# Roots on GpSimd, MLP token groups without shared buffers, early statistics for half of q, two halved tables, and transposes of h by DMA

## The chip, the cores and the metric

One core of a Trainium2 chip runs the kernel. The metric is the device time of one execution in microseconds. A core has five engines with queues of their own: TensorE (PE, with its weight loads shown apart as PEld), VectorE (DVE), ScalarE (ACT), GpSimd (POOL) and SyncE (SP), which here does nothing but issue DMAs. They meet only at semaphores.

## What is computed

A layer norm, a gated long convolution, and a mixer with an MLP, on 2048 tokens of 512 channels in bf16, one batch:

```python
h  = x + q_n * y,         x = q,  q_n = layernorm(q)
     kv = (causal 4-tap filter of k, per channel) * v
     y  = irfft(rfft(pad(kv)) * rfft(pad(ssm_k)))[:S] + kv * ssm_D
n  = layernorm(h)
g  = gelu(layernorm(n) @ w1)      # 512 -> 512
x1 = n + shifted(g) @ w2          # four channel quarters moved by +1, -1, +2, -2 tokens
h2 = gelu(layernorm(x1) @ w3) @ w4   # 512 -> 1792 -> 512
out = h + x1 + h2
```

## The kernel before

**Order by hand.** The kernel does not run its steps in the order of the code. Each call of `add`, `v` or `dma` appends a step to a list, with the engines that may run it (A for ACT, V for DVE, G for GpSimd, S for SP), an estimate of its duration and the names that it reads and writes. `Plan.issue` then emits the steps in the order of the numbers in `ISSUE` (L40 to L72); a number is the step's place in the list, and a letter behind it picks the engine where there is a choice. Every engine runs its own instructions in that order, so each engine's queue can be read off the string.

**Front.** k, v and the convolution kernel h (`ssm_k`) are loaded; k's tiles are transposed on PE, and the four taps are products with diagonal matrices (L399), accumulated in PSUM and multiplied by v on DVE (L404). Sixteen DMAs (L412) put these rows into the layout of the transform. Beside this, GpSimd, DVE and ACT make tables of sines and cosines: iota, a multiply and add (L306), an AND (L309), a sine (L313 to L320), and four DMAs scatter a table into `Wc` (L354). h is transposed on PE (L427) and evacuated into `Rh`.

**Transform.** Stage A (L446) transforms k and h in 16 blocks each; each block is cast from PSUM into `Tk` or `Th` on ACT (L161) or DVE (L163). Stage C (L470 to L473) gives spectra in 32 blocks, cast into `xt`; `product` (L586 to L593) multiplies the two spectra on DVE in eight chunks, the last two in halves. Then 16 blocks on PE (L647) are cast into `Gs`, and `last_level` (L702) gives y for two token tiles at a time.

**Norms.** q (a norm of 16 tiles) is loaded whole after h's buffer is free; DVE takes `bn_stats` and `bn_aggr` of each tile (L552, L553), and a Newton iteration of eight DVE instructions (L532 to L537), with one or two ahead and one behind, gives the reciprocal roots. ACT and DVE apply them (L632, L635). `gate` multiplies y by the normalized q, adds q and takes statistics; after every second pair of tiles `rsqrt_h` (Newton for two roots at once, since layer norm is applied twice) and four normalizations give `hn`; `on_pe` transposes it, two tiles at a time, and ACT or DVE evacuates it.

**MLP.** `gelu_mm` is one block of 128 hidden channels for 512 tokens: four matmuls of 512 columns and a gelu on ACT. `mix` adds the product with w2 to the normalized h (L834), takes statistics and a third set of roots, normalizes, and transposes: the first token group on PE, the other three by DMA from SP (L861). w3 and w4 follow for the token groups 2 to 5, 6 to 9, 10 to 13, and 14, 15, 0, 1.

**Buffers.** Large tiles share slots by tag (`slot`): a new tile in a slot waits for the readers of the old one. k, v and k's rows share C; in turn `Yp` and then the MLP's activations take it. y's scratch `ysb` lies in the tile of the weights, in the place that the output's scratch uses later; `x1` takes the slot of the normalized q.

Of the kernel before, what the change touches and what calls it, by code (L numbers as in the profile page):

```python
# [16 lines left out]
P = 128  # L17
# [23 lines left out]
25 3 0 5 7 4 1 2 49 9 26 8 11 29 24 21 6 50V 31 23 13 10 51 16 85 32G 14 22 52 12 20 86V 87 48 15 19 40 74 17 98  # L41
88A 27 34 46 108 35V 99A 37 75 91 109V 53 36 89 39 92 66 76G 28 102 67 90 33 97 100 93 103 62 18 128 30 94 57G
96 47 131 68 101 133 64 38 107 134 132V 104 42 69 105 95 44 63 106 65 77 118 78V 41 79 135V 110 80 54G 83 58 84
45 59 55 112 60 43 119V 129 70 113 71 73 72 111 136 130A 81 117 82 115 122 114 212 137A 120 123 56 61 200 121
138 210 179 201A 208 211V 186 126 209A 127 196 124 187V 197A 206 125 184 116 213 207A 185V 188 214 182 189A 183V
180 139 190 181A 204 202 140G 205V 191A 155 156A 203V 153 163 154A 147 164V 173 148A 174V 151 149 152A 167 141
169 150A 168V 171 170A 177 172V 159 178A 198 160V 175 199A 157 176V 158A 161 192 223 162A 165 239 257 166A 243
194 235 258 195A 261 224 241 193A 259 245 225 142 263 244 260V 265 262A 143 240 237 266A 273 219 144G 264A 275
221 217 277 274A 267 271 276A 289 238 268 272A 287 246 270 278A 283 215 290A 269 285 229 284A 297 280 288A 279
286A 295 236 282 298A 299 281 301 296A 233 313 291 302A 307 292 300A 309 230 294 314A 311 293 308A 242 304 310A  # L50
319 303 312A 321 222 306 325 320A 305 323 231 322A 315 326A 337 316 324A 331 234 317 338A 335 318 332A 333 218
327 345 336A 328 347 334A 343 227 346A 329 349 420 330 348A 385 363 366 226 340 365 344A 339 367 364 228 342
350A 341 145 352 146 351 220 354 353 232 396 216 355 247 356 394 397A 248 358 398 249 357 395A 250 360 359 399A
390 251 400 362 368 391A 252 361 392 253 401V 414 393A 406 254 407V 416 415A 404 417A 255 405V 410 402 411A 408
256 403V 388 409A 386 389V 387A 412 379V 421 413A 380V 371V 373V 370A 418 422 369V 382A 383V 374V 384V 430 378V
423A 372V 375V 381A 424 457 431A 425 428 376A 465 432 458A 426 433 466A 492 429 434 419 500 436 435 427 437 467
377A 438 493A 501A 527 459 441A 468 442A 460 443A 445 469 444A 463 535 446A 470 471 689 464 528A 461 447 472 462
494 448A 473 536A 455 502 477A 495 476A 503 479A 480 496 453 478A 537 481A 449 498 506 454 482 504 456 483A 507
499 451 497 505 538 450 508 486 452 488 487 490 541 512A 484 539 489 511V 491 529 515 485 474 568 530 516A 569
542 531 514A 513V 533 517 532 572 534 540 518A 439 475 543 521 525 440 546A 547V 509 570 522 550 510 571 526 523  # L60
551A 549V 519 548V 575 524 552 520 577 553A 573 595 578 574 579 556 581 554 557 580 576 582 583 558 555 560 559
592 596 585A 584V 561 597 587A 588 594 615 589A 586V 593 565 590 617 618 591A 600 601 544 616 714 562 716 566
715 567 564 692 545 717 563 598 696 693 599 604 690 605 602 698 647 699 697 691 704 649 708 619 705 603 712 606
709 706 713 702 707 607V 700 620 703 608 609V 710 701 648 610 694 711 623 650 627 695 624 613A 718 719 614 653
611V 621 612 625 622 626 628 629 630 651 631 652 659 657 734 658 660 728 671 632 655 735 633 736 654 723 729 738
634 635 672 724 673 674 675 676 636 637 638 645V 639A 643V 646 739 640 737 644 750 725 752 751 677 727 678 742
679 753 680 641V 720 730 642 743 726 748 731 656 722 661 662 732 663 721 685V 749 756 686 744 733 740 687V 745
761 688 754 741 664 746 665 755 666 667 668 788 669 747 670 681V 770 762 771 789 786 763 768 787 799 778 784 779
683V 769 684 757 682 785 764 765 824 758 780 825 759 794 772 781 760 782 773 766 783 774 767 792 775 790 793 776
791 818 777 826 819 804 827 806 805 828 807 820 829 830 821 812 831 800 813 814 801 808 815 822 809 810 816 811  # L70
823 795 817 833 796 832 798 802 803 797 838 834 837 836 835 842 839 841 840 843 844 845
# [3 lines left out]
class Plan:  # L75
# [5 lines left out]
    LAT = 0.2  # L81
# [40 lines left out]
def kernel(  # L122
# [48 lines left out]
    slot("C", [P, 24064], "kin")  # L171
    slot("S1", [P, DC, S], "hraw")
    slot("B", [P, 11776], "kta")
# [4 lines left out]
    def k_sb():  # L178
        return X["kin"][:, 0:9728].rearrange("p (r d) -> p r d", d=D)

    def v_sb():
        return X["kin"][:, 9728:15872].rearrange("p (b t d) -> p b t d", b=3, d=D)

    def Rk():
        return X["kin"][:, 15872:24064].rearrange("p (n d) -> p n d", d=2 * P)

    def kT():
        return X["kta"][:, 0:9728].rearrange("p (c r s) -> p c r s", c=DC, s=P)

    def dg():  # L190
        return X["kta"][:, 9728:11776].rearrange("p (c j s) -> p c j s", c=DC, s=P)
# [741 lines left out]
```

## Time and profile before

| | us |
|---|---|
| median of three runs (261.11 to 263.3) | 261.93 |
| profiled execution | 262.43 |
| its span, first to last instruction | 260.4 |

PE is busy for 227.0 us, DVE for 180.7, ACT for 152.7 and GpSimd for 30.0. Mean durations of single instructions, ns:

| what | engine, line | ns, count |
|---|---|---|
| Tk, Th, xt, Gs casts, 128x1024 from PSUM | ACT L161 | 1034 to 1064 |
| the same | DVE L163 | 1187 to 1231 |
| product, 128x2048 | DVE L586 | 1213, 12 |
| statistics of a tile, aggregate | DVE L552, L553 | 677 to 681, 163 to 170 |
| normalization of a tile | ACT L740, DVE L635 | 805, 406 |
| gelu block | ACT L772 | 596, 56 |
| matmul of 512 columns | PE L768 | 383; successive ones start 216 apart |
| eight transposes of h or x at full clock | PE L756 | 455 for eight in the chain of waits |
| iota in three levels | GpSimd L302 | 3510, 3120 |
| iota in two levels | GpSimd L505 | 1035, 2 |
| multiply and add, 128x1024 int32 | GpSimd L306 | 1307, 2 |
| product, 128x2 | GpSimd L495 | 508, 2 |
| DMA transpose: SP held, landing | SP L861 | 1214, 2.4 us |
| load of q: two DMAs issued at 45.2 and 45.9 | SP L522 | first statistics at 58.97 |

Durations of successive instructions on one engine overlap a little: four statistics take 2.36 us in the chain of waits, not 2.72. A group's duration is from dispatch to end, so the distance between starts is the better price for a row of equal ones.

### The profile page before, as it was taken

Reading aid. Unit: us, or ns where it says so; the run is one execution under the profiler, and the core shown is the slowest. Engines: PE = TensorE matmul, PEld = TensorE weight load, DVE = VectorE, ACT = ScalarE, POOL = GpSimd, SP = SyncE. Lnnn points to the kernel's source line nnn. Section 1 sums busy time; section 2 is a strip of 40 time slices with the busy share of each in tenths; the row PEclk is TensorE's granted clock in tenths of the full one; section 3 lists DMA queues with packets and bytes.
Section 4 is the critical chain, followed back from the end, with each engine's and each line's share of the span. In section 5 each row is a group of like instructions: output and inputs, shape, how many; then the busy total and the mean of one; then the engine's idle time right before and its main releaser. Section 6 shows DMA issues by size and latency. Waiting matters only on the chain.

```text
span 260.4 us, 4761 instructions
## 1 busy us (share of the span) xinstructions
PE 227.0 (87%) x1933; PEld 148.4 (57%) x1946; DVE 180.7 (69%) x410; ACT 152.7 (59%) x194; POOL 30.0 (12%) x37
## 2 busy tenths in 40 slices
PE   2959998989987929657699999999999999999993
PEld 2859998869987918523345454444444444444441
DVE  8895849979999999999999964897290421001341
ACT  2618158997989969999887664524163307604000
POOL 8989200303000000000000000000000000000000
PEclk9986999797999988997799999999999999999999
DMA  6986494970000079200000000020450021000141
GB/s 186 359 320 202 130 256 126 199 149 3 3 1 3 0 269 381 81 0 0 0 3 0 1 0 4 20 60 0 63 123 19 20 63 40 0 0 3 26 95 41
DMA packets 25044, 21.15 MB, mean 81 GB/s; under 512 B 14655, under 2 KB 21823, under 8 KB 24894
## 3 DMA queue, kind: packets, MB, share of 16 engines
q1 hardware_dynamic: 25022, 20.85, 28.7%
q8 instruction: 15, 0.25, 0.4%
q14 instruction: 7, 0.06, 0.1%
HBM read 13.50 MB, written 2.10 MB: 60 GB/s over the span
## 4 chain that ended last, share of the span: by engine, by line
PE 49%; DVE 23%; issue 1%; ACT 1%
PE pw L768 24%; PE p L890 18%; DVE Yp L586 7%; PE p L828 5%; DVE bst L552 3%; DVE Gs L163 2%; DVE Yp L590 2%; DVE Yp L593 2%; PE pt L756 2%; DVE qn L635 1%; DVE wts L711 1%; DVE hh L713 1%; ACT hh L740 1%; DVE mvq L553 1%; DVE xt L163 0%
## 5 line engine op out<-in xcount | busy, mean ns | idle before, releaser
L768 PE MATMUL pw<-act,wts 128*128 128x512 bf16 x285 | 65.3, 383 | 1.5 <-ACT act L161 1.3
L772 ACT ACTIVATE g<-pw 128x512 bf16<-128x512 f32 x56 | 32.5, 596 | 48.9 <-PE pw L768 48.9
L890 PE MATMUL p<-wts,g 128*128 128x512 bf16 x217 | 48.8, 379 | 0.3
L768 PEld LDWEIGHTS <-wts 128*128 128x128 bf16 x288 | 28.4, 99 | 35.4 <-issue 3.1
L895 DVE TENSOR_TENSOR wts<-p,wts 128x1024 bf16<-128x1024 f32 (+1 forms) x9 | 9.9, 1106 | 54.2 <-PE p L890 48.4
L890 PEld LDWEIGHTS <-g 128*128 128x128 bf16 x224 | 21.9, 98 | 26.4
L399 PE MATMUL psh<-kta 128*128 128x128 bf16 x256 | 17.7, 239 | 3.1 <-ACT tta L313 3.1
L586 DVE TENSOR_TENSOR Yp<-xt 128x2048 bf16<-128x2048 bf16 (+1 forms) x20 | 19.3, 999 | 0.0
L399 PEld LDWEIGHTS <-kta 128*128 128x128 bf16 x256 | 17.2, 108 | 3.3 <-issue 3.3
L161 ACT CAST xt<-pch 128x1024 bf16<-128x1024 f32 x16 | 16.1, 1041 | 2.4 <-PE pch L473 1.5
L470 PE MATMUL pck<-Tk,Wc 128*128 128x256 bf16 x64 | 16.1, 290 | 1.6 <-ACT xt L161 1.3
L472 PEld LDWEIGHTS <-Wc 128*128 128x128 bf16 x128 | 14.8, 115 | 2.8 <-issue 2.8
L161 ACT CAST xt<-pck 128x1024 bf16<-128x1024 f32 x15 | 15.2, 1034 | 1.0 <-DVE Yp L586 1.0
L834 DVE SCALAR_TENSOR_TENSOR x<-hh,rho,p 128x512 bf16<-128x512 bf16 x16 | 11.7, 739 | 5.5 <-PE p L828 5.5
L470 PE MATMUL pch<-Th,Wc 128*128 128x256 bf16 x64 | 14.7, 272 | 0.9 <-ACT xt L161 0.7
L473 PEld LDWEIGHTS <-Wc 128*128 128x128 bf16 x128 | 14.8, 115 | 0.5
L828 PE MATMUL p<-wts,act 128*128 128x512 bf16 x61 | 14.8, 379 | 0.2
L404 DVE TENSOR_TENSOR kvq<-psh,kin 128x1024 bf16<-128x1024 f32 x8 | 9.7, 1220 | 7.6 <-PE psh L399 7.6
L470 PEld LDWEIGHTS <-Wc 128*128 128x128 bf16 x128 | 14.8, 115 | 0.1
L473 PE MATMUL pck<-Tk,Wc 128*128 128x128 bf16 x64 | 14.7, 229 | 0.0
L472 PE MATMUL pck<-Tk,Wc 128*128 128x128 bf16 x64 | 14.7, 229 | 0.0
L647 PE MATMUL pg<-CSG,Yp 128*128 128x128 bf16 x128 | 9.3, 236 | 5.8 <-DVE Yp L590 5.1
(130 smaller groups left out, 407.1 us busy)
## 6 DMA issues: line engine op xcount, KB each, us to landing
wts<-in_B_w_dram SPq DMA_DIRECT2D x2, 1792.0 KB, 10.1
kin<-in_A_k_dram SPq DMA_DIRECT2D x4, 512.0 KB, 7.1
kin<-in_A_v_dram SPq DMA_DIRECT2D x4, 512.0 KB, 6.9
hraw<-in_A_ssm_k_dram SPq DMA_DIRECT2D x4, 512.0 KB, 9.0
kin<-kvq SPq DMA_DIRECT2D x16, 128.0 KB, 3.3
q_sb<-in_A_q_dram SPq DMA_DIRECT2D x2, 1024.0 KB, 10.6
out_dram<-wts SPq DMA_DIRECT2D x14, 128.0 KB, 2.3
Wc<-tta SPq DMA_DIRECT2D x4, 384.0 KB, 5.6
```

The source lines that it names most:

```text
L161: A.copy(o, src)
L399: T_.matmul(pv[:, i, c * P:(c + 1) * P], lhsT=kT()[:, c, t0 + i + 3 - j, :], rhs=dg()[:, c, j, :], start=(j == 0), stop=(j == 3))
L470: T_.matmul(pv[:, kk, :, :].rearrange("p r d -> p (r d)"), lhsT=W[0], rhs=Tw.rearrange("p r d -> p (r d)"), start=True, stop=False)
L472: T_.matmul(pv[:, kk, 0, :], lhsT=W[1], rhs=Tw[:, 1, :], start=False, stop=False)
L473: T_.matmul(pv[:, kk, 1, :], lhsT=W[2], rhs=Tw[:, 0, :], start=False, stop=True)
L586: v(0.08 + 1.14 * s, lambda i=i: V.tensor_tensor(out=pr(i), in0=x(0), in1=x(1)[:, i:i + 1].to_broadcast([P, 2, n, 8]), op=MUL), ["C"] + rx ...
L768: T_.matmul(ps[:], lhsT=wt(w)[:, k, m * P:(m + 1) * P], rhs=xT()[:, k, 4 * b * P:(4 * b + 4) * P], start=(k == 0), stop=(k == DC - 1))
L772: add({"A": 0.59}, lambda: A.activation(dst(), X[pkey][:], ACT.Gelu_apprx_tanh), r + [pkey, "gelu"], [key])
L828: T_.matmul(ps[:, i, :], lhsT=gT()[:, m, t + i + 2 + off[m], :], rhs=wt("w2")[:, m, :], start=(m == 0), stop=(m == 3))
L834: v(0.74, lambda t=t, i=i, key=key: V.scalar_tensor_tensor(out=X["x1"][:, t + i, :], in0=hn()[:, t + i, :], scalar=rho[:, t + i:t + i + 1] ...
L890: T_.matmul(ps[:, i, :], lhsT=X["g2"][:, b % 2, m, s0:s0 + P], rhs=wt("w4")[:, m, :], start=(m == 0), stop=(m == FC - 1))
L895: v(0.62 * (hi - lo), lambda j=j, lo=lo, hi=hi, key=key: V.tensor_tensor(out=obb()[:, j, lo:hi], in0=X[key][:, lo:hi], in1=ofb()[:, j, lo: ...
```

## The change

- **Roots.** `newton` and `chain` are gone. `root` is four GpSimd instructions for a group of tiles: variance plus epsilon, a power of -0.5 against a constant tile, the negated mean, and its product with the root. `roots_h` has four more for `rho` (two of them an addition and another power). The roots of q are taken for four tiles at a time.
- **q.** `EARLY` is 8: two DMAs copy the first eight tiles of q into the space of k's first rows once those are transposed, and the statistics of these tiles read that copy. q is still loaded whole later for the gate. Normalizations of q and h may run on GpSimd; the order puts eight of q's there (tiles 0, 1, 2, 4, 5, 6, 12, 15), seven on ACT and one on DVE.
- **Buffers.** y is evacuated into h's own rows and gated in place, `ysb` is gone, `x1` overwrites `hn` in place, and v has four buffers instead of three.
- **Tables.** The table for `Wc` is computed for half of its entries; the other half is the first times a sign per partition (`sgnF`). The second table of the last level is no longer computed by iota, AND and sine: DVE negates the first (one instruction), and four DMAs move halves across partitions.
- **k.** The four loads are aligned to the token tiles, without a halo; the tap products of the first tiles read the last three tiles one token earlier through a column of zeros ahead of each transposed tile. 64 transposes remain of 76.
- **Transposes of h.** For the token groups 1 to 3 of h (`BY_DMA`) four DMA transposes per group from SP replace 16 transposes on PE and two evacuations.
- **Order.** `ISSUE` is new as a whole.

```diff
+    def power(r, var, n, rk, wk):
+        pool(0.33 + 0.165 * n, lambda: G.tensor_tensor(out=r, in0=var, in1=half[:, 0:n], op=OP.pow), ["half", rk], [wk])
+
+    def root(mv, var, r, nm, n, rk, key, add2=None):
+
+        kv, kr, km = (key + (x,) for x in "vrm")
+        if add2 is None:
+            pool(0.25, lambda: G.tensor_scalar(var, mv[:, :, 1], EPS, None, op0=ADD), rk, [kv])
         else:
+            pool(0.25, lambda: G.tensor_scalar(var, mv[:, :, 1], *add2, op0=MUL, op1=ADD), rk, [kv])
+        power(r, var, n, kv, kr)
+        pool(0.25, lambda: G.tensor_scalar(nm, mv[:, :, 0], -1.0, None, op0=MUL), rk, [km])
+        pool(0.22, lambda: G.tensor_tensor(out=nm, in0=nm, in1=r, op=MUL), [kr], [km])
...
+    for h in range(2 if EARLY else 0):
+        dma(0.3 * EARLY, lambda h=h: nc.sync.dma_start(
+            k_sb()[h * N1:(h + 1) * N1, 0:EARLY, :], qd[h, :, 0:EARLY, :]),
+            r=("C",), w=[("k", t) for t in range(EARLY)])
...
+    v(0.6, lambda: V.tensor_scalar(flat2(kvqt[1][:]), Wf[:, 0].rearrange("p n k -> p (n k)"), -1.0, None, op0=MUL),
+      wfs, [("kvq", 1, 0), ("kvq", 1, 1)])
     for hf in range(2):
...
+                nc.sync.dma_start(flat2(kvqt[0][:])[64 * h:64 * h + 64, x], src[64 - 64 * h:128 - 64 * h, x])
...
+    for a in range(3):
+        v(0.4, lambda a=a: V.tensor_scalar(plane(a, 1), plane(a, 0), sgnF, None, op0=MUL),
+          ["A", "pf", ("t", a, 0)], [("t", a, 1)])
...
+        y = lambda: hs()[:, 2 * u:2 * u + 2, :]
...
+            for i in range(4 if b in BY_DMA else 0):
+                add({"T": 1.3}, lambda t=4 * b + i: nc.sync.dma_start_transpose(
+                    xT()[:, :, t * P:(t + 1) * P], hn()[:, t, :]), ["C", "B", ("hn", 4 * b + i)], [("xT", 4 * b + i)])
...
+    def x1():
+
+        return hn()
```

The new order, decoded for the stretches that matter (numbers of tiles, blocks or groups behind the names):

- SP: k rows 0, `shift_k`, k 4, k 12, k 8, `ssm_D`, v0, v1, h3, h1, early q (first half), h0, h2, early q (second half), row copies of quarter 1 (two), v3, two more, v2, row copies of quarter 0 (four), the four scatters, the eight row copies of quarters 3 and 2, q (two), four pieces of the second last-level table, w3, w2, w4, w1, transposes of h 4, 5, 7, 6, 8, 9, 11, 10, 13, 14, 12, 15.
- DVE at the end of stage A: a cast of Tk4, statistics of q15, a cast of Tk10, statistics of q11 and q12, the negation, a cast of xt, statistics of q13, the first product. Among the products: an xt cast and the statistics of q14 and q8. After them: six Gs casts, q10, one normalization, q9, four aggregates, then the gates in the order 2, 3 (tiles 4 to 7), 0, 1, with 4 and 5 behind the statistics of 0 to 3.
- ACT from the last Gs cast: a normalization of q, y2, y3, q3, y0, the table for gelu, y1, y4, q9, q10, q8, q11, y5, hn4 to hn7, q13, y7, hn2, hn0, hn1, y6, hn9, the evacuation of h0's transposes, and the first gelus of w1.
- GpSimd from the last product on: qn1, qn2, qn0, part of a root of q, qn5, qn4, qn6, qn12, the root of q8 to q11, the roots of groups 1, 0 and 2 of h, the powers of `rho` for groups 2 and 1, the root of group 3, the rest of `rho`, then the roots of x1.
- PE: y blocks 2, 3, 0, 1, 4, 5, 7, 6; the transposes of h2; w1 block 0 of group 1; the transposes of h0; then w1 blocks of groups 1 and 0, of group 2, and products with w2 between them.

More of the change, by code (lines that the diff above doesn't have):

```diff
@@ L525 @@
     vq = cst.tile([P, NT], F32)
+    varq = cst.tile([P, NT], F32)
     bst = cst.tile([P, NT, 6], F32)
[L527 to L537 removed]
@@ L539, in chain, with pool @@
-    def chain(fns, r, w, whole):
-        fns = list(fns)
-        if whole:
-            def fn():
-                for f in fns:
-                    f()
-            v(0.2 * len(fns), fn, r, w, lat=0.1)
-        else:
-            for i, f in enumerate(fns):
-                v(0.08, f, r if i == 0 else (), w, lat=0.12)
+    half = cst.tile([P, 16], F32)
+    add({"G": 0.1}, lambda: G.memset(half[:], -0.5), w=["half"])
+    def pool(us, fn, r=(), w=(), lat=0.1):
+        add({"G": us}, fn, r, w, lat=lat)
@@ L564 @@
+    for t0 in range(0, NT, 4):
+        q_stats(t0)
     slot("C", [P, 24064], "Yp")
```

363 lines of the change are left out of this document (178 added, 185 removed).

## The prediction

> **What bounds the kernel now.** I read first the chain of waits, which says on which engine each stretch ends, then the busy time by stretch, cut where that chain and the timelines change their work, then the timelines of single engines.
>
> By stretch (start:end, length, then busy PE, PEld, DVE, ACT, POOL, granted clock, DMA share, GB/s):
>
> ```profile
> 0.00:41.20 41.20, 32.42 (x474) 31.38 (x476) 30.46 (x47) 18.39 (x18) 25.48 (x33) 0.92 0.78 237
> 41.20:59.00 17.80, 15.18 (x251) 13.18 (x248) 15.20 (x15) 17.39 (x19) 2.26 (x2) 0.89 0.72 157
> 59.00:66.85 7.85, 7.85 (x91) 7.42 (x89) 7.85 (x16) 6.33 (x8) 2.24 (x2) 0.82 0.01 2
> 66.85:101.00 34.15, 26.57 (x344) 25.81 (x341) 34.12 (x68) 29.72 (x32) 0.00 (x0) 0.95 0.26 90
> 101.00:107.50 6.50, 5.18 (x82) 4.75 (x81) 6.50 (x11) 6.50 (x8) 0.00 (x0) 1.00 0.74 262
> 107.50:127.10 19.60, 11.58 (x81) 5.72 (x81) 18.92 (x60) 18.92 (x25) 0.00 (x0) 0.90 0.00 1
> 127.10:256.30 129.20, 128.24 (x624) 60.09 (x636) 66.95 (x201) 55.48 (x89) 0.00 (x0) 0.99 0.13 28
> 256.30:260.40 4.10, 0.00 (x0) 0.00 (x0) 0.65 (x1) 0.00 (x0) 0.00 (x0) 0.92 0.13 32
> ```
>
> Three kinds of stretch: to 41.2 nothing is full (loads, tables, k's taps); from 41.2 to 127.1 VectorE (DVE) and ScalarE (ACT) are both nearly full, DVE to the last percent from 59 to 107.5; from 127.1 PE is full. GpSimd (POOL) is empty from 66.85 on. The chain of waits (start, length, what) shows which DVE work carries the middle:
>
> ```profile
> 97.88 0.09 DVE rq L532
> ...
> 106.96 1.67 DVE qn L635 x6
> 108.63 0.18 issue
> 108.81 1.70 DVE qn L635 x5
> ...
> 125.35 0.17 DVE nb L727
> 125.52 0.02 issue
> 125.54 1.53 ACT hh L740 x2
> 127.07 0.05 issue
> 127.12 1.03 PE pt L756 x8
> 128.15 2.74 PE pw L768 x8
> ```
>
> The roots (L532 on), eleven normalizations of q and the second group's root, 123.54 to 125.52, all stand in the chain; PE becomes full only when that group's normalized rows reach its transposes. One more view, the timeline of all engines early on, because the change puts GpSimd beside DVE:
>
> ```profile
> 12.47 1.83 POOL L334 MEMSET Wc<- 128x1024 uint32 x2
> 12.56 2.29 DVE L306 TENSOR_SCALAR tta<-tta,pf 128x1024 int32<-128x1024 int32 x1 [1.05 <-POOL tta L302]
> 14.27 1.52 POOL L302 IOTA tta<- 128x1024 int32 x1
> 14.78 1.04 DVE L360 TENSOR_SCALAR mk<-mk 128x4 f32<-128x4 f32 x1
> ```
>
> L306 takes 0.81 us elsewhere, and L360 writes four numbers: both end with, or 0.5 us after, the GpSimd instruction that was running.
>
> **The change, stretch by stretch.** The profiled execution took 262.43 us (span 260.4 and 2.0 around it), 0.5 over the median of 261.93; the sum is made against 262.43. Durations that follow are distances in the chain, a little under the means.
>
> *To the start of stage A (41.2 now).* PE is busy 32.42 us behind a first wait of 5.2. Twelve of 76 transposes of k go (7.1 us for 76: -1.1), giving 36.5 if the other waits go too (0.5 for the halo's memset, which is removed; 3.1 before 18.43, when DVE's first tap product ends behind table work, 15.97 to 17.24, of which half is removed). Against it, SP's queue now holds the early copy of q (1 MB; at the 320 to 359 GB/s of the loads, 3 us) ahead of h0, h2, v3 and v2, and its first half waits for the transposes of k's rows 0 to 7, with h0 and h2 queued behind. The eight early statistics (0.69 each with their aggregates, 5.5) lie in DVE time that is free (30.46 of 41.2 busy, and the evacuations of Rh go to ACT); with that cover gone they would cost 5.5. Bounds: -6 (clock at full) and 0 (v2, v3 late). I take -4, nearest to the counted 36.5 with a microsecond of waits.
>
> *Stage A to the first product (41.2 to 66.85, 25.65).* Now 20 casts on ACT (0.93), one sine, then eleven statistics of q before the first product. After: 18 on ACT (16.7), 14 on DVE (1.14, 16.0), three statistics, the negation of Wf (0.6) and one xt cast: ACT 16.7 + 3 x 0.92 = 19.5, DVE 16.0 + 1.8 + 0.6 + 1.1 = 19.5. Two waits are added. Seven of the last eight row copies now leave after the last tap product (0.62 apart, about 3 to land: 7.5 us), and stage A has only twelve h blocks (6.2) to cover that. And q's first late statistic stands on DVE ahead of a cast of Tk: q landed 17.8 after this point before, and DVE gets there at 14.8; behind it wait the last Tk block and all of k's stage C. They overlap; I take +2, so 21.6: -4. Bounds -6 and -1.
>
> *Products (66.85 to 101).* Six full ones (2.34 + 0.63 + 0.60) and four halves (1.17 + 0.37 + 0.34) are 28.9; the rest of 34.1 is five statistics (3.0), 13 aggregates (1.2), one AND (0.6) and six root steps (0.55). After: 28.9, two statistics, four aggregates, one xt cast (1.11): 31.6, so -2.5. ACT's 30 casts (27.6) stay under it. Then six Gs casts on DVE in place of five: 6.8 for 6.5, +0.3. The eight normalizations on GpSimd (a price no row has: the nearest, 128x1024 from SBUF at 1.21 to 1.42, halved, is 0.6 to 0.7; the whole 1.4 is the other bound) start after the last product and have the 6.8 of Gs casts and 2.5 more as cover.
>
> *Gates to a full PE (107.5 to 127.1, then 129.2).* DVE loses 3.4 of normalizations and two roots of 2.0, and gains 1.9 (two statistics, one normalization, four aggregates). It no longer ends this stretch; ACT does: from the end of the Gs casts its queue is y2 (done at 2.5), y3, one qn, y0, the table load (1.4), y1, y4, four qn (0.72 each), y5, hn4 to hn7 (2.9), a qn, y7, hn2, hn0, hn1: 18.8. y6 follows, and hn9, which needs the third root: statistics done at 18.4, root at 20.3. The evacuation of the first group's transposes stands behind it, to 22.0. By then PE has done 2.6 us of this stretch's work, so it is full as from 19.4, against 19.6 before. The DMA transposes cost PE nothing: six groups of eight (0.455) go, two (h0 to h3) now fall inside, -1.8, and w1's first block, +0.9, falls inside too. Each DMA transpose holds SP 1.2 and lands in 2.4: four end 6.0 after the first. hn4 is ready at 12.8, so 18.8 for w1's first block, which waits about 1 us in time counted above; the fourth group's end at 34.4 where PE comes at 35.9. Together -1.1. Bounds: -4.3 (DVE's end taken, 17.1) and +2.
>
> *GpSimd's roots.* Per group of h, eight instructions in place of DVE's thirteen, four of them on the way to the normalized rows. The nearest rows are a two-column product (0.39 and 0.63) and 0.32 to 0.61 for tensor_scalar on 17 to 64 columns: with those, 4 x 0.32 to 4 x 0.63, 1.3 to 2.5 us, where DVE takes 2.0; I use 1.9, the middle. How long a POW is, no row shows (last rival). DVE work beside it: no row shows a two-input SBUF operation (gates, products) next to GpSimd arithmetic, so the price of meeting it is 0 to the whole GpSimd instruction; I take +0.5 in all, between the statistics at 61.4 (0.60 apart beside a 1.03 us iota, untouched) and L306 above.
> The Trainium skill, in "SBUF — State Buffer", section "Who interferes with whom", says that a DVE instruction with two SBUF inputs shuts out a GpSimd instruction that reads SBUF, and the reverse, for the whole instruction. By that rule the time would be that of the first rival below; the trace agrees for tensor_scalar (2.29 for 0.81) and shows nothing for two inputs.
>
> Sum: -4 -4 -2.5 +0.3 -1.1 +0.5 = -10.8, so 251.6; against the median 251.1. I say 251.5.
>
> **Rivals.** *Port held (chance 0.15).* Every root instruction near a product or gate holds DVE for its length: two q roots among the products (3.5), the first normalization against the last two product steps (1), three h roots (5.2): +9 over the 0.5, 260 at worst, 257 if half of it falls on statistics, which the trace shows untouched. For: L306. Against: DVE has about 1.5 us of slack behind ACT in the gates.
>
> *Front late (0.15).* The early copy delays v2 and v3 and q lands 3 us later: front 0, stage A -1: +7, 258.5. For: DMA is 0.78 busy up to 41.2. Against: the Wc scatter can leave some 4 us before its 31.2, as an iota (3.12) and a multiply (1.42) of GpSimd ahead of it are gone.
>
> *Transposes don't pay (0.05).* If four DMA transposes take 2.4 each in a row (9.6, not 6.0), the second group's end at 22.4 and PE waits 2.6, the third's 0.5: 254.5. For: two of the twelve held SP for 2.0. Against: the median is 1.2.
>
> *Slower: POW is long (0.08).* GpSimd's queue is in order: behind h2's root stand the POWs of rho for groups 2 and 1, then h3's root. With p per POW, h1, h0 and h2 follow each other from 8.4; at p = 5, h2's root ends at 25.8 for 20.3, two rho chains end at 37 and h3's root at 43 for 28.1; PE comes at 35.9 and waits to 49.5: +13.6, which uses up the 10.8. So from p of about 4.5 it is slower; at 6, 270. Against: GpSimd arithmetic on 17 to 64 columns takes 0.6 at most.
>
> **Numbers.** Forecast 0.57, with 245 to 255 as its own range. About 1% (2.6 us) is what a measurement of this kernel tells from no change, so faster means under 259.3: the forecast, the transposes, most of the port and the front, 0.87; same 0.06; slower 0.07. The range of 8 in 10 is 245 to 258.
>
> **What would show it.** Right: stage A begins near 37, products begin near 59 and last 32, PE is full about 19 us after the last Gs cast, DVE free of roots. Wrong: DVE rows of products or gates stretched beside GpSimd; DVE idle on q's load before the last Tk cast; PE waiting on DMA before w1's blocks; POW above 2 us.

## The result and the profile after

The changed kernel takes 265.26 us (median of 20 runs, 262.28 to 268.5), the kernel before 262.39 on the same chip (20 runs, 260.97 to 263.43); the ratio is 1.0067 (95% interval 1.0037 to 1.0096). It was forecast at 251.5 and comes out slower, by 0.7% (0.4 to 1.0). (The ratio leaves out runs that lie over 1.5% above the fastest of their kernel, so it is nearer to 1 than the ratio of the two medians.) The profiled execution took 264.27, its span is 262.4.

Busy time by stretch, kernel after, cut at the same events as before (start:end, length, busy PE, PEld, DVE, ACT, POOL, granted clock, DMA share, GB/s):

```profile
0.00:47.40 47.40, 30.95 (x480) 29.46 (x481) 28.20 (x54) 23.98 (x20) 23.42 (x34) 0.95 0.94 220
47.40:64.40 17.00, 13.72 (x216) 11.59 (x216) 15.49 (x18) 15.09 (x16) 3.11 (x7) 0.63 0.97 179
64.40:69.80 5.40, 5.29 (x73) 5.22 (x73) 5.34 (x8) 4.86 (x7) 0.00 (x0) 1.00 0.11 24
69.80:103.50 33.70, 28.40 (x362) 27.93 (x361) 32.49 (x48) 28.45 (x32) 0.57 (x1) 0.91 0.25 83
103.50:110.95 7.45, 6.03 (x90) 5.42 (x88) 7.17 (x7) 6.54 (x8) 6.81 (x12) 0.95 0.89 285
110.95:130.30 19.35, 9.23 (x71) 4.91 (x72) 18.30 (x45) 18.70 (x25) 8.66 (x16) 0.86 0.14 28
130.30:258.30 128.00, 127.14 (x588) 58.27 (x598) 53.42 (x111) 49.80 (x84) 17.94 (x42) 0.98 0.18 37
258.30:262.40 4.10, 0.00 (x0) 0.00 (x0) 0.67 (x1) 0.00 (x0) 0.00 (x0) 0.86 0.13 32
```

The first stretch is longer by 6.2 although PE and DVE have less to do in it (ACT has more, 23.98 for 18.39, and is idle for half of it); its DMA share has gone from 0.78 to 0.94 while the rate fell from 237 to 220 GB/s. What the other stretches win is less than that:

| from the traces, us | before | after | difference | predicted |
|---|---|---|---|---|
| first cast of Th (stage A) | 41.22 | 47.44 | +6.2 | -4 |
| stage A to first product | 25.6 | 22.4 | -3.2 | -4 |
| first to last product | 34.1 | 33.6 | -0.5 | -2.5 |
| last product to last Gs cast (on ACT) | 6.8 | 7.5 | +0.7 | +0.3 |
| last Gs cast to PE's end | 148.5 | 147.3 | -1.2 | -0.6, with +0.5 for GpSimd |
| span | 260.4 | 262.4 | +2.0 | -10.8 |

(ACT's last Gs cast of the kernel before ends at 107.77; the stretches are cut at 107.5.)

The chain of waits of the kernel after, its front (start, length, what):

```profile
3.14 9.62 DMA dcol<-in_A_ssm_D_dram
...
12.77 18.22 DMA kin<-in_A_q_dram
...
31.01 0.59 SPq L430
...
32.30 6.85 DMA kin<-kvq
...
48.72 5.70 DMA kin<-kvq
...
55.17 1.23 DVE Tk L163
```

The early copy of q carries the chain from 12.77 to 31. SP is tied to it too: the row copy at 31.01 is the eighth DMA behind the copy's second half, and SP issues it as that half lands; the row copy ahead of it had left at 28.3. What DVE does meanwhile is in its timeline (start, length, line, what, in brackets the idle time before it and who ended it):

```profile
22.91 1.22 DVE L422 TENSOR_TENSOR kvq<-psh,kin 128x1024 bf16<-128x1024 f32 x1
31.08 1.88 DVE L576 BATCH_NORM_STATS2 bst<-kin 128x6 f32<-128x512 bf16 x3 [6.95 <-DMA kin<-in_A_q_dram]
...
35.52 1.22 DVE L422 TENSOR_TENSOR kvq<-psh,kin 128x1024 bf16<-128x1024 f32 x1 [0.65 <-DMA kin<-kvq]
...
47.46 1.23 DVE L163 CAST Th<-pah 128x1024 bf16<-128x1024 f32 x1 [2.84 <-DMA Wc<-tta]
```

The statistics stand in DVE's queue ahead of the fifth tap product: DVE waits 6.95 for the copy and does six of them before that product. But they are not what ended last before it. The product writes into the buffer of quarter 1, and the last row copy of that quarter landed at 35.24, 0.4 after the last of the six; SP had issued it at 23.58, as the first half of the early copy landed. So the loss goes through SP and the DMA engines, and DVE's wait for q lies beside it. The same holds for stage A: its casts wait for the scatter of `Wc` (`Th` takes the slot of the tables that the scatter reads). SP issued the scatter from 34.0 on (31.2 before), as the load of v3, eight DMAs ahead of it, landed at 33.96, and the scatter was complete 13.3 later (9.4 before). So the net loss lies in the front. The question for the experiments was why the copy does this.

### The profile page after: what moved, and what is told of

Read it like the earlier page. It is cut to its first block, busy times and chain, and to the rows that moved or that the text cites. A ratio compares the mean times of both kernels' runs of the same rounds, so it can differ in the third digit from the quotient of the medians.

```text
span 262.4 us, 4615 instructions
## 1 busy us (share of the span) xinstructions
PE 220.8 (84%) x1874; PEld 142.8 (54%) x1886; DVE 161.1 (61%) x287; ACT 147.4 (56%) x185; POOL 60.5 (23%) x110
## 4 chain that ended last, share of the span: by engine, by line
PE 56%; DVE 19%; DMA 15%; SPq 3%; ACT 3%; issue 2%; POOL 1%; DVEq 0%; ACTq 0%
PE pw L792 24%; PE p L919 18%; DMA kin<-in_A_q_dram 7%; PE p L858 5%; DMA kin<-kvq 5%; DVE Yp L616 5%; DMA dcol<-in_A_ssm_D_dram 4%; DVE Tk L163 3%; DVE bst L576 3%; PE pg L674 2%; SPq L430 2%; DVE hh L741 1%; DVE Gs L163 1%; DVE kvq L422 1%; DVE Yp L623 1%
## 5 line engine op out<-in xcount | busy, mean ns | idle before, releaser
L576 DVE BATCH_NORM_STATS2 bst<-hh 128x6 f32<-128x512 bf16 x32 | 20.7, 678 | 0.0
L417 PE MATMUL psh<-kta 128*128 128x128 bf16 x256 | 15.2, 220 | 2.2 <-DVE kvq L422 2.2
L662 POOL TENSOR_SCALAR qn<-q_sb,rq,vq 128x512 bf16<-128x512 bf16 x8 | 6.4, 807 | 43.1 <-ACT Gs L161 43.0
L864 DVE SCALAR_TENSOR_TENSOR hh<-hh,rho,p 128x512 bf16<-128x512 bf16 x16 | 11.3, 741 | 8.0 <-PE p L858 4.8
L417 PEld LDWEIGHTS <-kta 128*128 128x128 bf16 x256 | 14.5, 98 | 2.6 <-issue 2.3
L488 PE MATMUL pck<-Tk,Wc 128*128 128x256 bf16 x64 | 14.6, 273 | 1.0 <-ACT xt L161 1.0
L490 PEld LDWEIGHTS <-Wc 128*128 128x128 bf16 x128 | 14.5, 113 | 1.3 <-issue 1.3
L161 ACT CAST xt<-pck 128x1024 bf16<-128x1024 f32 x14 | 14.1, 1028 | 1.8 <-PE pck L491 1.8
L488 PEld LDWEIGHTS <-Wc 128*128 128x128 bf16 x128 | 14.5, 113 | 0.1
L491 PEld LDWEIGHTS <-Wc 128*128 128x128 bf16 x128 | 14.5, 113 | 0.0
L796 ACT ACTIVATE act<-pw 128x512 bf16<-128x512 f32 x16 | 9.4, 596 | 9.0 <-PE pw L792 9.0
L674 PE MATMUL pg<-CSG,Yp 128*128 128x128 bf16 x128 | 10.3, 254 | 4.6 <-DVE Yp L620 4.3
## 6 DMA issues: line engine op xcount, KB each, us to landing
wts<-in_B_w_dram SPq DMA_DIRECT2D x2, 1792.0 KB, 10.6
```

The costliest lines, as they stand in the source:

```text
L161: A.copy(o, src)
L417: T_.matmul(pv[:, i, c * P:(c + 1) * P], lhsT=kT()[:, c, r % NT, s0:s0 + P], rhs=dg()[:, c, j, :], start=(j == 0), stop=(j == 3))
L488: T_.matmul(pv[:, kk, :, :].rearrange("p r d -> p (r d)"), lhsT=W[0], rhs=Tw.rearrange("p r d -> p (r d)"), start=True, stop=False)
L490: T_.matmul(pv[:, kk, 0, :], lhsT=W[1], rhs=Tw[:, 1, :], start=False, stop=False)
L491: T_.matmul(pv[:, kk, 1, :], lhsT=W[2], rhs=Tw[:, 0, :], start=False, stop=True)
L576: v(0.68, lambda: V.bn_stats(bst[:, t, :], x(t)), r, [("bst", t)], lat=0.08)
```

## The experiments

Times are medians; each ratio is against runs of the kernel before on the same chip (261.9 to 262.3 there). Differences are of medians; where the ratios say something else, both are given. Steps are named by tile or block: kvq 30 is the first tap product of quarter 3.

**Is it the copy?** In e1_no_copy the two DMAs are no steps any more, and the statistics of tiles 0 to 7 read the rows of k that lie there:

```diff
-        dma(0.3 * EARLY, lambda h=h: nc.sync.dma_start(
-            k_sb()[h * N1:(h + 1) * N1, 0:EARLY, :], qd[h, :, 0:EARLY, :]), ...
+        add({"-": 0.0}, lambda: None)
```

> The changed kernel without the two DMAs that copy half of q early; the statistics of tiles 0 to 7 read k's rows instead, so these numbers are not q's. Theory A (the copy crowds the front: it took 15.5 us to land, and h0, h2, v2, v3 and the row copies came late behind it): without it v3 and v2 land before 30, the first Th cast comes at 38 to 42 instead of 47.4, and the time falls by 5 to 8 us, to 256 to 260. Theory B (the front is late through GpSimd's order and its meetings with DVE, such as a six-column cast of 3.70 us and a multiply of 3.36): the first Th cast stays at 45 or later and the time falls by under 2 us.

261.08, ratio 0.9966 (0.9924 to 1.0008): the copy costs 4.2 (2.7 by the ratios), between the two theories. But the first Th comes at 44.9, not before 41.2, and the last tap product even later (43.6 for 43.1). The profiled execution was the slowest of ten (264.42), so these two times are late; still they point to something else that had been hidden.

e2_copy_wide moves the same bytes in another shape, two transfers of 128 partitions by four tiles (so the statistics are of other tokens than the partition's own):

```diff
-            k_sb()[h * N1:(h + 1) * N1, 0:EARLY, :], qd[h, :, 0:EARLY, :]),
+            k_sb()[:, 4 * h:4 * h + 4, :], A_q[0].rearrange("(p t) d -> p t d", t=NT)[:, 4 * h:4 * h + 4, :]),
```

> The changed kernel with the early copy in the same places and of the same 1 MB, but as two DMAs over 128 partitions and four tiles each instead of 64 partitions and eight tiles; the tokens are others, so the statistics are of other rows. Theory A1 (bytes and places in the queue decide): both copies land about 15 us after issue, and the time stays within 1.5 us of the changed kernel's. Theory A2 (the shape decides: 64 partitions take one side of the memory): they land in under 10 us, the first Th cast comes 3 us or more earlier, and the time falls by 2 to 4 us.

262.62, ratio 1.000 (0.9959 to 1.004): 2.6 less than the kernel after (1.8 by the ratios, whose intervals just meet); the copy lands in 11.4 where it took 15.5, and the first Th comes at 44.3 for 47.4.

e3_before_copy adds the copy (and nothing that waits for it) to the kernel before, behind its loads of h3 and h1:

```diff
+    for h in range(2):
+        dma(2.4, lambda h=h: nc.sync.dma_start(<free space of Rk, 64 partitions>, qd[h, :, 0:8, :]))
```

> The kernel before with the same 1 MB copy of q added among its loads (behind the loads of h3 and h1, as in the changed kernel), into space that the row copies of k use later; nothing reads it. Theory A: its first Th cast moves from 41.2 to 45 to 48 and the time rises by 4 to 7 us, to 266 to 269. Theory B: under 1.5 us more.

265.15, ratio 1.0114 (1.0064 to 1.0164): the first Th moves from 41.2 to 43.4. That lies between the two theories; about 3 is paid by the other transfers alone, with no statistics that wait for the copy.

e4_copy_late issues the copy behind v and the row copies of quarter 0, its statistics behind the last tap product (SP: ... rows 010, **early q0, early q1**, scatters).

> The changed kernel with the early copy moved on SP's queue behind the loads of v and the row copies of quarter 0, and its statistics and aggregates on DVE behind the last tap product. Theory A: tap products end by 38 instead of 44.2, as h0, h2, v3 and v2 no longer stand behind the copy; the scatter and the last row copies now do, so part is given back: first Th cast 42 to 45, time 259 to 263. Theory B: first Th cast at 45 or later, time within 1.5 us of the changed kernel's.

266.7, ratio 1.0208 (1.0146 to 1.0271): no gain, as theory B said (1.4 over the kernel after). The copy now meets the scatters, which land in 10.6 (7.1), and the first Th comes at 51.3.

**What else makes the front late?** In e1_no_copy, DVE and GpSimd met (timelines of e1_no_copy, the three table operations on DVE and what GpSimd runs):

```profile
20.33 1.39 DVE L316 TENSOR_SCALAR kta<-kta,pf 128x1024 int32<-128x1024 int32 x1
21.64 2.18 DVE L364 TENSOR_SCALAR tta<-tta,pf 128x1024 bf16<-128x1024 bf16 x1
23.74 1.25 DVE L362 TENSOR_SCALAR tta<-tta 128x1024 bf16<-128x1024 bf16 x1
```

```profile
21.70 5.62 POOL L344 MEMSET Wc<- 128x1024 uint32 x5
```

Alone, L316, L364 and L362 take 0.81, 0.48 and 0.42. With the copy these five memsets had been held back to 28.46, because they stand behind GpSimd's addition of D to h0 and h2 and the copy kept those two to 28.3: the copy hid this second fault. e6_memsets is e1_no_copy with the seven memsets moved ahead; e5_rows tests a rival, SP's order of the last row copies, on the kernel after; e7_both joins the two:

```diff
 GpSimd (e6, e7): ... iota Wf u1
+memset Wc 3, 11, 6, 7, 1, 2, 5
 dcol add 1, ..., dcol add 0
-memset Wc 3, 11, 6, 7, 1, 2, 5 (between and behind the two)
 PE, DVE, SP (e5, e7):
-taps, kvq, v of quarter 3 before quarter 2; its row copies mixed
+taps, kvq, v of quarter 2 before quarter 3; its row copies ahead of quarter 3's
```

> Everything is computed as in the kernel after; only the order of two quarters of tokens is changed: tap products, row of v, and the four row copies of quarter 2 now come ahead of those of quarter 3, so that four of the eight last row copies can be issued about 4 us before the last tap product instead of behind it. Theory 'the row copies are late by their place in SyncE's queue': first cast of Tk from 55.2 (kernel after) to 51 or 52, the first late statistic of q from 64.4 to 61, first product from 69.8 to 67, time 2 to 3 below the kernel after (262 to 263 where it has 265.3). Rival 'the front is late, the queue is not': the last tap product stays at 43.1, the rows land 10 us after it however they are ordered, Tk at 54.5 or later, time within 0.7 of the kernel after.

> Statistics of q's tiles 0 to 7 are taken from the rows of k that lie in the buffer (the early copy of q is left out, as in e1_no_copy, which has 261.08 and kvq 01 at 27.5), and the seven memsets of Wc that stood behind the two additions of D to h on GpSimd now stand ahead of them. Theory 'GpSimd's memsets meet DVE's table work': the memsets run at 16 to 22, DVE's L316, L319, L362 and L364 go back to 0.4 to 0.9 each, kvq 01 at 24 or before, the last tap product at 40 to 41 (43.6), first cast of Th at 42 (44.9), first product at 68 (69.9), time 1.5 to 2 below e1_no_copy, about 259.3. Rival 'they meet elsewhere': the memsets then stretch the mask products and the dg multiplication before 20, kvq 10 is later by what kvq 01 gains, time within 0.5 of 261.1.

> As e6_memsets (statistics of q's tiles 0 to 7 from rows of k, no early copy, memsets ahead) and with the order of quarters of e5_rows. Theory 'copy, memsets and row copies are the three causes of the late front': the gains add: last tap product at 40, first Th at 42, first Tk at 49, first late statistic at 59, first product at 65 (66.85 before, 69.83 after), time 256 to 257.5, some 8 below the kernel after. Rival 'stage A is held by work on DVE and ACT, not by its rows': first Tk moves with the rows, the first product stays at 68 or later, time 259 or more.

e5_rows: 265.06 (kernel after 265.26), ratio 1.0178 (1.011 to 1.0247), first Tk at 55.4 (55.2): nothing gained, as the rival said, though the last tap product came at 47.0 for 43.1, so here the order of the rows was not tested by itself. e6_memsets: 258.34, ratio 0.9882 (0.9843 to 0.9921); kvq 01 at 23.0, last tap product at 37.7, first Th at 41.7, first product at 64.05, all earlier than in e1_no_copy and than was expected. The time is 2.7 less than there (2.2 by the ratios). e7_both: 259.0, ratio 0.9907 (0.988 to 0.9935): nothing on top of e6_memsets, so the order of the rows is no cause on a front without the two faults either; my hope of 256 fell. In e6_memsets the timeline of GpSimd reads:

```profile
14.63 7.12 POOL L344 MEMSET Wc<- 128x1024 uint32 x7
21.73 0.35 POOL L515 TENSOR_TENSOR hraw<-hraw,dcol 128x2 bf16<-128x2 bf16 x1
```

Most of them now run while DVE waits for PE's first tap blocks, though L364 and L362 still take 1.25 each; the additions end at 23.1 for 21.8 in e1_no_copy.

**Can the statistics be early without the cost?** e9_memsets_copy keeps the copy and moves only the memsets. e10_all_late has no copy and takes all statistics from q itself, three of the eight before the first product and five among the products (`if t < EARLY` becomes `if t < 0`). e11_wide computes all that the kernel after does: memsets ahead, the copy in e2's shape behind h0 and h2, and, as the 16 tokens of a partition are the same in both layouts and only the partition's number differs, two small DMAs that move means and variances:

```diff
-                stats(lambda t: k_sb()[:, t, :], mvq, t, ["C", ("k", t)], "mvq")
+                stats(lambda t: k_sb()[:, t, :], mvn, t, ["C", ("k", t)], "mvq")
...
+    for h in range(2):
+        dma(0.5, lambda h=h: nc.sync.dma_start(mvq[h * N1:(h + 1) * N1, 0:8, :], mvn[h:P:2, :, :]))
 SP: ... h3, h1, h0, h2,
+early q0, early q1, rows 110, ..., rows 201, mvq 0, mvq 1, q0, q1
```

> The kernel after, early copy and all, with only the seven memsets of Wc moved ahead of the two additions of D on GpSimd. It completes a square: copy and old order 265.3, no copy and old order 261.1, no copy and new order 258.3. Theory 'two causes that hide each other': with the copy the memsets were held back to 28.3 by the late h0 and h2 and so met little table work; moved ahead they cost DVE nothing, but the front is still held by the copy, so the time stays at 264 to 265.5 and the first cast of Th at 46 or later. Theory 'the causes add': 2.7 below the kernel after, 262.5, first Th at 44.

> No early copy, memsets ahead, and the statistics of q's tiles 0 to 7 taken from q itself once it is loaded: three of them before the first product, five among the products (the change without its early half of the statistics). Theory 'DVE is full from 58 to 108, so each statistic costs its own length': three of 0.69 plus aggregates, 2.4, put the first product at 66.4 (64.05 in e6_memsets), five of 0.62 plus aggregates 3.5 more by the last product: 258.3 + 5.5, 263.5 to 264. Rival 'half of them fall into DVE's waits in stage A and among the products': 260 to 261.5.

> Memsets ahead, and the early copy in another form: two transfers of 128 partitions by four tiles (in the token order of k's rows; the same 16 tokens lie on one partition, so that two transfers of 4 KB each put mean and variance on q's partitions), issued behind h0 and h2 in place of around them. Theory 'the copy hurts by its shape and place': h0 and h2 land at 20 to 23 as without it, first Th at 42 to 43, first product at 64.5 to 65.5, time 258.5 to 260.5. Theory 'the copy hurts by its bytes': 1 MB more in a stretch where the DMA engines are 0.8 to 1.0 busy costs 3 us wherever it stands: first Th at 44.5, product at 67, time 261 to 262.5.

e9_memsets_copy: 265.37, ratio 1.0115 (1.0067 to 1.0162): with the copy as it was, the memsets don't matter. So the memsets bring 2.7 without the copy and nothing with it, and the copy costs 7.0 with the memsets ahead and 4.2 with them behind: one fault hid the other. e10_all_late: 262.82, ratio 1.0058 (1.0008 to 1.0108): 4.5 more than e6_memsets (by its stages 2.3 between stage A and the first product and 2.7 among the products), so the early half of the statistics is worth about 4.5 if its data come free. e11_wide: **258.35**, ratio 0.9899 (0.9857 to 0.9942): it beats both kernels, the one before by 1%, and its copy costs nothing against e6_memsets. Its stretches:

```profile
0.00:39.70 39.70, 31.27 (x480) 29.95 (x481) 31.36 (x56) 23.88 (x20) 25.00 (x34) 0.96 0.90 256
39.70:58.80 19.10, 14.35 (x229) 12.11 (x226) 15.54 (x16) 15.89 (x17) 3.12 (x7) 0.73 0.91 172
58.80:64.88 6.08, 4.79 (x65) 4.74 (x64) 5.39 (x7) 4.06 (x6) 0.00 (x0) 1.00 0.23 48
64.88:98.50 33.62, 28.13 (x367) 27.53 (x365) 32.44 (x48) 28.37 (x31) 0.53 (x1) 0.95 0.23 78
98.50:105.55 7.05, 5.35 (x87) 4.81 (x84) 7.00 (x7) 6.44 (x8) 6.86 (x12) 1.00 0.96 307
105.55:125.00 19.45, 9.83 (x71) 5.00 (x72) 18.29 (x45) 18.80 (x24) 8.81 (x17) 0.81 0.14 29
125.00:252.20 127.20, 127.15 (x600) 58.18 (x598) 53.40 (x111) 49.59 (x84) 17.87 (x42) 0.99 0.18 37
```

Against the kernel after, the first stretch is 7.7 shorter (39.7 for 47.4) at 256 GB/s for 220, and the products are as long as they were (33.6).

**Shape or place of the copy?** e11_wide changed both. Four kernels, all with the memsets ahead: e13_narrow_behind (64 partitions by eight tiles, behind h0 and h2), e14_wide_ahead (e11's copy around h0 and h2, as in the kernel after), and two that part the shape's two properties, behind h0 and h2: e17_narrow_4kb and e18_wide_8kb.

```diff
 e17:
+            for g in range(2):
+                nc.sync.dma_start(k_sb()[g * N1:(g + 1) * N1, 4 * h:4 * h + 4, :], qd[g, :, 4 * h:4 * h + 4, :])
 e18, once:
+            k_sb()[:, 0:EARLY, :], A_q[0].rearrange("(p t) d -> p t d", t=NT)[:, 0:EARLY, :]
```

> As e9_memsets_copy (265.37), with the early copy in its old form, two transfers of 64 partitions by eight tiles, but issued behind h0 and h2 as in e11_wide (258.35). Theory 'place': h0 and h2 no longer stand behind it, first Th at 40 to 42, time 258.5 to 260. Theory 'shape': the copy still takes 15 us or more to land and holds v3, v2 and the row copies behind it, last tap product at 42 or later, time 263 to 265.5.

> As e11_wide (258.35), with the wide copy at the place of the kernel after, its first half ahead of h0 and h2 and its second behind them. Theory 'place': h0 and h2 late again, time 261.5 to 263. Theory 'shape': the copy lands in 11 to 12, first Th at 40 to 42, time 258 to 259.5.

> As e13_narrow_behind (264.75), with the same 1 MB to the same places in four transfers of 64 partitions by four tiles in place of two of 64 by eight, so that a run of consecutive bytes is 4 KB, as in e11_wide, in place of 8 KB. Theory 'the long runs': the rate between 15 and 20 stays near 400 GB/s (131 to 147 in the kernel after), first Th at 40 to 42, time 258.5 to 260. Theory 'half the partitions': landing in 15 or more, first Th at 46 or later, time 263.5 to 265.5.

> As e11_wide (258.35), with the 1 MB in one transfer of 128 partitions by eight tiles, 8 KB runs. Theory 'the long runs': the rate falls under 200 GB/s while it runs, first Th at 44 or later, time 262 or more. Theory 'half the partitions': the rate stays near 400 GB/s, first Th at 39.5 to 42, time 258 to 259.5.

| copy | time (runs) | ratio | lands in | GB/s, 18 to 20 us |
|---|---|---|---|---|
| e13: 64 partitions, 8 KB runs | 264.75 (4) | 1.0114 (1.0071 to 1.0157) | 16.9 | 137 |
| e17: 64 partitions, 4 KB runs | 262.1 (10) | 0.9964 (0.9914 to 1.0013) | 11.6 | 201 |
| e18: 128 partitions, 8 KB runs | 259.02 (5) | 0.9885 (0.9803 to 0.9967) | 12.8 | 418 |
| e11: 128 partitions, 4 KB runs | 258.35 (10) | 0.9899 (0.9857 to 0.9942) | 11.8 | 380 |
| e14: as e11, around h0 and h2 | 259.46 (10) | 0.9927 (0.9893 to 0.9961) | 11.2 | 408 |

(From 18 to 20 the copy is at least partly in flight, beside the last loads of h; the DMA share is 1.01 to 1.05 in all five.) The place costs a microsecond at most (e14 against e11, and 0.6 for the narrow copy, e9 against e13), the shape six (e13 against e11). Of the shape, both properties count: e17 lies between the two theories. By the medians the long runs cost 2.7 at 64 partitions and half the partitions 3.7 at 4 KB, by the ratios 3.9 and 1.7, so which is the larger is open; at 128 partitions long runs cost 0.7 at most. (Runs of e17 go from 258.96 to 264.63, and the profiled one is its fastest. Its four transfers also alternate between the two halves of the partitions, which no run tests alone.)

Busy time by stretch shows the loss as a rate, not as idle engines; the kernel after, then e11_wide:

```profile
10.00:15.00 5.00, 4.63 (x65) 4.51 (x63) 2.59 (x3) 4.17 (x4) 4.53 (x5) 1.00 0.99 383
15.00:20.00 5.00, 5.00 (x93) 5.00 (x91) 3.85 (x6) 4.97 (x5) 0.00 (x0) 1.00 1.02 189
```

```profile
15.00:20.00 5.00, 5.00 (x91) 4.90 (x90) 4.44 (x5) 4.71 (x4) 5.00 (x6) 1.00 1.02 400
```

Both have a DMA share of 1.02, and one moves half of what the other does. The other loads suffer too: the four of h landed in 12.4 to 16.2 in the kernel after and in 9.7 to 11.5 in e1_no_copy. The Trainium skill, "DMA: Bandwidth & Descriptors", section "Rules for kernel authors", says that two transfers to disjoint partition halves share the same engines and don't run beside each other, and advises one transfer of 128 partitions; the runs agree with the advice (264.75 and 262.1 against 259.02 and 258.35). Why half the partitions lower the rate is not shown by any run.

**The other parts.** e8_pe_transposes puts the transposes of h's groups 1 to 3 back on PE (`BY_DMA = ()`, six groups of transposes and six casts of DVE at their places); e12_qn_dve puts GpSimd's eight normalizations of q on DVE (eight letters G become V), on e9_memsets_copy.

> The kernel after with the transposes of h's groups 1 to 3 back on PE: six groups of eight transposes and six casts of DVE in place of twelve DMA transposes. Theory 'the transposes pay': first groups in PE's idle time before PE is full, four of the six groups (0.455 each) in the full stretch: PE's end 1.8 later, and the six casts (about 0.68 each) on DVE, two of them in the stretch before PE is full, add 0.3 to 1; time 1.8 to 3 above the kernel after (267 to 268.3). Rival 'a transpose on PE is hidden, DMA transposes only move a wait': time within 0.7 of the kernel after; PE's idle time in the full stretch shrinks by what the transposes add.

> As e9_memsets_copy, but the eight normalizations of q that the change gave to GpSimd are done by DVE, at their places between the casts of Gs and the gates. Theory 'GpSimd's normalizations pay': eight of 0.28 to 0.41 on a full DVE push its last Gs cast and the gates back; the way from the first product to PE's end, 188.5 in the kernel after, is 1.3 to 2.5 longer. Rival 'ACT ends this stretch anyway, and GpSimd's 0.8 each only moves the work': 188 to 189, time within 0.7 of e9_memsets_copy.

264.78, ratio 1.0126 (1.0053 to 1.02), and 265.3, ratio 1.0113 (1.0021 to 1.0206): no difference to the kernel after and to e9_memsets_copy (265.37) in the time. The front could hide it: in e8_pe_transposes, with the front of the kernel after, stage A began 2.3 earlier. The way from the first product to PE's end, which the front can't touch, was 189.5 and 188.6 where the kernel after has 188.4 and e9_memsets_copy 187.3; but over the kernels that don't differ there it goes from 186.9 to 188.7, so only the first stands out. e15_wide_qn_dve and e16_wide_pe_transposes repeat both edits on e11_wide:

> As e11_wide (258.35), with GpSimd's eight normalizations of q on DVE. In e12_qn_dve the way from the first product to PE's end was 188.6 against 187.3 in e9_memsets_copy, but the time the same. Theory 'they pay': 1 to 2 more than e11_wide, 259.4 to 260.4, the way from the first product to the second group's transposes (57.9 in e11_wide) 1 to 1.5 longer. Rival 'they only move work': 258 to 258.9, the way within 0.5.

> As e11_wide (258.35), with the transposes of h's groups 1 to 3 back on PE and their casts on DVE. In e8_pe_transposes the way from the first product to PE's end was 189.5, in the kernel after 188.4, in e11_wide 187.3. Theory 'the DMA transposes pay': four groups of 0.455 in PE's full stretch, 1.5 to 2 more than e11_wide, 259.9 to 260.4. Rival 'hidden': 258 to 258.9.

e15_wide_qn_dve: 260.23, ratio 0.9941 (0.9908 to 0.9975), 1.9 over e11_wide, though the two intervals touch; the way is 188.6 for 187.3. e16_wide_pe_transposes: 261.7, ratio 0.9994 (0.9964 to 1.0025), 3.3 over e11_wide; the way is 189.2 for 187.3, and the rest lies ahead of the first product, where the edit is not. The single stage that holds an edit says more than the whole way:

| from the traces, us | normalizations on DVE (e12, e15) | transposes on PE (e8, e16) | the other kernels with the change |
|---|---|---|---|
| last product to last Gs cast | 8.4, 8.4 | 7.0, 7.0 | 7.0 to 7.7 |
| last Gs cast to PE's end | 146.6, 146.6 | 148.9, 148.9 | 146.6 to 147.5 |

So both parts pay: the DMA transposes 1.6 (e8 against the kernel after) and 2.3 (e16 against e11), and GpSimd's normalizations 1.4 in both pairs.

## Why the prediction was wrong

**Start of stage A, -4 predicted, +6.2 measured: the failed step.** I costed the copy as bytes ("1 MB; at the 320 to 359 GB/s of the loads, 3 us"). The loads of the trace were of 128 partitions, and I took their rate for a copy of 64: its halves landed 12.8 and 18.2 after their issue, and from 15 to 20 all DMA traffic was 189 GB/s. For the other shape the price was right: the last of h's loads and of the copy is in at 20.5 without a copy (e6_memsets), at 23.8 with the wide one (e11_wide, 3.3 later) and at 30.6 with the narrow one (e13_narrow_behind, 10.1 later). I also left out who waits behind it: SP's queue is in order, so v3, v2, the row copies and the scatter all came late, and with them the tap products and stage A. The early statistics, which I put at nothing since "they lie in DVE time that is free", did wait for their data, but the row copies ended later, so no run shows that they cost anything.

The rival *Front late* had the cause and its place, at a chance of 0.15, but its price for the front (0, from v2 and v3 alone) was too low by 6. Its counter-argument, that the scatter could leave earlier, failed: 34.0 for 31.2, since SP stood behind the copy. The hidden second cause, memsets meeting table work, is the row that I showed myself (2.29 for 0.81); I never asked where the twelve memsets would fall once GpSimd's order changed.

With both repaired, stage A still begins at 39.7 (e11_wide) where I forecast 37. I had counted PE's work. But in every kernel with the change the first cast of Th comes 0.1 to 0.2 after the last piece of the scatter lands, so the scatter is what ends last there; in e11_wide it leaves 2.6 earlier than in the kernel before (28.6 for 31.2, where I had counted on some 4) and needs 11.0 for 9.4. Why it needs longer is open.

**Stage A to the first product, -4 predicted, -3.2 measured.** Right in its parts: casts and statistics moved as counted, and the wait for the last row copies, taken as 2, is there (Tk at 55.2, 12.1 after the last tap product starts). With the front repaired (e11_wide) the same wait keeps this way at 25.2: stage A begins at 39.7, but its first Tk comes at 48.7, 10.8 after the last tap product. So of this gain, too, the repaired kernel keeps only 0.5.

**Products, -2.5 predicted, -0.5 measured: mis-sized.** I took each aggregate and root step out at its own length. Timelines of DVE, kernel before and kernel after, one chunk each:

```profile
83.86 2.34 DVE L586 TENSOR_TENSOR Yp<-xt 128x2048 bf16<-128x2048 bf16 x2
86.12 0.18 DVE L553 BATCH_NORM_AGGREGATE mvq<-bst 128x2 f32<-128x6 f32 x1
86.24 0.69 DVE L590 TENSOR_TENSOR Yp<-Yp 128x1024 bf16<-128x1024 bf16 x1
86.85 0.68 DVE L593 TENSOR_TENSOR Yp<-Yp 128x1024 bf16<-128x1024 bf16 x1
87.45 0.17 DVE L553 BATCH_NORM_AGGREGATE mvq<-bst 128x2 f32<-128x6 f32 x1
87.64 1.23 DVE L586 TENSOR_TENSOR Yp<-xt 128x2048 bf16<-128x2048 bf16 x1
```

```profile
82.67 2.36 DVE L616 TENSOR_TENSOR Yp<-xt 128x2048 bf16<-128x2048 bf16 x2
85.06 0.69 DVE L620 TENSOR_TENSOR Yp<-Yp 128x1024 bf16<-128x1024 bf16 x1
85.68 0.68 DVE L623 TENSOR_TENSOR Yp<-Yp 128x1024 bf16<-128x1024 bf16 x1
86.46 2.36 DVE L616 TENSOR_TENSOR Yp<-xt 128x2048 bf16<-128x2048 bf16 x2
```

A chunk took 3.78 with two aggregates in it (83.86 to 87.64), and takes 3.79 without any (82.67 to 86.46). That such small steps stand in waits which dependent DVE instructions have anyway fits these distances, though no run tests it alone. The nine aggregates and six root steps are 1.4 by my sum; with a wait of 0.56 for ACT's cast of xt (at 77.87), which I had put under DVE's work, they make up the 2.0 that is missing.

**Gs casts, +0.3 predicted, +0.7 measured**, and **gates and PE, -0.6 with GpSimd's share, -1.2 measured**: together -0.5 for -0.3. ACT's queue was counted rightly (its third normalization after the group's root ends 18.6 after the last Gs cast, for 18.8), but it does not end this stretch alone. The chain of waits of the kernel after comes from DVE's gates and the root on GpSimd:

```profile
124.57 0.17 DVE mvh L577 x2
...
125.99 1.01 POOL rh L562
...
127.07 0.21 POOL nb L573
127.30 0.82 ACT hh L764
128.17 1.03 PE pt L780 x8
```

ACT's instruction before ends at 127.15, so the two ways are level to 0.15. The root takes 2.45 here (124.82 to 127.27), where I had taken 1.9.

**GpSimd.** POW is 1.04, far under the 4.5 from which it would have decided, so that rival falls. *Port held* falls too: timelines of GpSimd and of DVE in the kernel after:

```profile
113.15 1.05 POOL L562 TENSOR_TENSOR rq<-varq,half 128x4 f32<-128x4 f32 x1
...
119.17 0.55 POOL L570 TENSOR_SCALAR vh<-mvh 128x4 f32<-128x4 f32 x1 [3.90 <-DVE mvh L577]
119.80 1.36 POOL L562 TENSOR_TENSOR rh<-vh,half 128x4 f32<-128x4 f32 x1
```

```profile
119.00 0.66 DVE L741 TENSOR_TENSOR hh<-hh,qn 128x1024 bf16<-128x1024 bf16 x1
119.58 1.29 DVE L743 TENSOR_TENSOR hh<-hh,q_sb 128x1024 bf16<-128x1024 bf16 x2
```

Beside two gates GpSimd's POW is stretched from 1.05 to 1.36; the gates, 0.66 and 0.65 each, are as short as before. The meeting costs GpSimd, which had the time but for the 0.15 above. The rule that I cited from "SBUF — State Buffer" in the Trainium skill is seen on GpSimd's side alone, and there for 0.31, not for the gates' whole length. The row that I put beside it, 2.29 for 0.81, did not bear on it: that DVE operation has one tensor input.

*Transposes don't pay* falls with e8_pe_transposes and e16_wide_pe_transposes.

## What to carry to other kernels

A step that is moved early is free only if its data come free: price a new transfer by a row of its own shape, not by its bytes, and look up who stands behind it in the queue that issues it. When taking one thing away gains little, look in that trace for a second cause that it had kept apart from its victim. Read a small edit of a late stage from the stage that holds it: here one and the same front began stage A at 45.1 in the profile of one kernel and at 47.4 in that of another, and hid what the edit brought.

## What the runs showed of the hardware that I had not expected

- While 1 MB went to 64 partitions at a time, all DMA traffic fell to 137 to 201 GB/s (18 to 20 us) with all DMA engines shown busy; the same megabyte to 128 partitions ran at 380 to 418.
- SP issued a DMA only when the one eight places ahead of it had landed: in the kernel after at 12.77 (landed 12.76), 23.58 (23.56), 25.90 (25.88) and 31.01 (30.99). So one slow transfer holds up the eighth behind it, whoever needs that.
- Small DVE steps (an aggregate, shown as 0.17) between dependent products cost nothing: 3.78 for a chunk with two, 3.79 with none.
- DVE's gates, with two SBUF inputs, kept their length next to GpSimd's arithmetic (0.66 to 0.70 beside it, 0.66 to 0.68 alone), and GpSimd's gave way instead (1.05 to 1.36 for a POW on 128x4).
